# A finer order list for a gated linear attention fused with a Fourier-mix block, on one core

## The chip, the cores and the metric

The kernel runs on 1 core of one Trainium2 chip. The metric is the device time of one execution in microseconds (us). Three runs of the kernel before gave 525.32, 524.19 and 524.56 us, median 524.56.

A core has five engines that run at the same time, each through its own queue in order: PE (TensorE, matrix products into PSUM; its weight loads are shown as PEld), DVE (VectorE), ACT (ScalarE), POOL (GpSimd) and SP, which issues most of the DMA transfers. An engine waits for another one only at a semaphore, where it needs that engine's result or a buffer that the other still uses.

## The reference

Inputs q, k, v and f_logit have shape (4, 8, 768, 48): batch, heads, tokens, channels. The weights are 384 x 1536 and 1536 x 384, given in float64.

```python
# attention: a gated outer-product state for each head
f = 1 / (1 + exp(-f_logit))
for t in range(S):
    state = f[t, :, None] * state + outer(k[t], v[t])
    y[t] = q[t] @ state
# bridge: (B, H, S, D) -> x of (B, S, H*D) = (4, 768, 384)
mixed = real(fft(fft(x, axis=tokens), axis=channels))
u = x + mixed
un = (u - mean(u)) / sqrt(var(u) + 1e-6)        # over the channels
out = u + relu(un @ w_ch1) @ w_ch2
```

## The kernel before

**Units and batches.** The attention is cut into 16 units: unit u is batch u // 4 and the head pair u % 4. Each batch then has its Fourier part and its two-layer part. Work of neighbouring batches overlaps: while PE works on the layers of one batch, the units of the next one run beside them.

**The order is written out by hand.** The program text holds one string, ORDER, of words separated by blanks. A loop at the end of the kernel takes them one by one, and each word issues one piece of work. Nothing reorders it afterwards: an engine's queue is the sequence in which the words issued its instructions. The order of words on different engines doesn't matter in itself, only through waits. Most pieces come from Python generators: a word advances its generator to the next `yield`. The words are:

- a number n: the next step of unit n's attention. The steps are: gate logarithms (ACT, L372 and L373); the cumulative scan (DVE, L379); exponentials (ACT, L383, L384 and L387); two multiplications (DVE, L391 and L392); score products (PE, L400); the causal mask (DVE, L404); products of the diagonal parts with the values and the far scores with their copy (PE, ACT L579); the other value products and the state products `ds` (PE, L559 and L599); the state scan (DVE, L607); the state's share of the output (PE, L616) with five copies (ACT, L625 to L629); transposes `yt` (PE, L636) with two copies into x (ACT, L640 and L641); and the folds of x for the Fourier part (DVE, L663 to L669, for later head pairs L678 to L687 as well, of which `se` at L681 is the first transform's operand).
- Kn: the key transposes of unit n (PE, L538, with one copy on ACT).
- Fb: the next step of batch b's Fourier part: four transforms along the tokens, `z` (PE, L724, with copies on ACT), then three mixes along the channels, `mix` (PE, L743), added to x by DVE.
- Hb: the next step of its normalization: moments (DVE), and `turn`, a subtraction (DVE, L779), three transposes (PE, L782) and a copy (ACT, L783).
- Pb: the next step of the two layers. For batch 0 the first layer is 36 plain groups `up` (L871), with one pair's second layer `po` (L880). For batches 1 to 3 each of three pairs of token blocks has 15 products of the first layer (`hidden`, PE L840). DVE first makes sums of the inputs (L814) for some of them; the result goes to h by a copy on ACT (L847) or an accumulation on DVE (L849), and some end in a relu (ACT, L851). Eight steps of the second layer follow, `fx` and `fz` (PE, L894).
- r, R (three at once): a DMA of a raw weight block into one of three buffers. C: its conversion to float32 (ACT L281, DVE L283 and L284, POOL L285), 24 in all. W and B: sums of weight blocks (DVE). V and c: the raw weight blocks are read again and their smallest magnitudes found (DVE, L344). M: a verdict from these and from the scans' extremes, on which a second, slower path would run; the inputs here don't take it.
- Ln with letters: DMA loads of unit n's f, k, q and v. I, Z, i: constants. T: the DMA loads of the Fourier tables (SP, and an indirect load on POOL, L226). S: their sorting (POOL, L240 to L252; L240 and L241 finish the table that `z` reads).
- D: eight spare bfloat16 products on PE (L192). Their result isn't used and they wait for no other engine's data except once for a constant.

**Buffers.** PSUM tiles of the attention come from a ring of two (tag sc), those of the Fourier part and of most of the layers from another ring of two (tag f), and all units share one output bank y, so a unit's first value products wait for the copies of the unit before.

Of the kernel before, what the change touches and what calls it, by code (L numbers as in the profile page):

```python
# [12 lines left out]
C = 128  # L13
# [70 lines left out]
def kernel(  # L84
# [23 lines left out]
    R = 64 + D  # L108
# [256 lines left out]
    def attention(u, x_all):  # L365
# [18 lines left out]
        nc.scalar.activation(W, W, AF.Exp)  # L384
        te = te_t[u % 2][:R]
# [5 lines left out]
        nc.vector.tensor_tensor(Q, Q, g, ALU.mult)  # L391
        nc.vector.tensor_tensor(g, W, K, ALU.mult)  # L392
# [149 lines left out]
    def outputs(u, x_all, AT, Q, K, te, T=None):  # L542
# [26 lines left out]
        if te is not None:  # L569
# [3 lines left out]
            for i in range(NCH // 2):  # L573
                for p, c in ((0, i), (64, i + 3)):
                    for r in range(2):
                        nc.tensor.matmul(ps[p:p + 64, r, i * 64:i * 64 + 64],
                                         lhsT=K[ROWS[r], c * C:c * C + 64],
                                         rhs=Q[ROWS[r], c * C + 64:(c + 1) * C], start=True, stop=True)
            nc.scalar.copy(far, ps[:, :, :NCH // 2 * 64].rearrange("p r (c t) -> p r c t", t=64))  # L579
# [534 lines left out]
```

## Time and profile before

| | |
|---|---|
| median of the runs | 524.56 us (524.19 to 525.32) |
| the profiled execution, first to last instruction | 526.3 us |
| PE busy | 494.9 us (94%) |
| DVE busy | 378.3 us (72%) |
| ACT busy | 218.4 us (42%) |
| POOL busy | 58.8 us (11%) |
| first product of the first transform | 59.54 us |
| last DVE instruction of the last conversion ends | 117.6 us |
| last product ends | 519.4 us |
| mean granted PE clock | 0.974 |

The profile is one execution, recorded by the hardware. Its span, 526.3 us, is 1.7 us over the median of the timed runs. In a row of the timeline stand the start, the duration, the engine, the line of the program, the operation, its tiles and shapes, and in brackets the idle time of the engine before it with what ended it. PE's ends are modelled, so that products that overlap count as busy throughout.

### The profile page before, as it was taken

The numbers are of one execution on the slowest core, as the hardware profiler recorded it, in microseconds if no ns is written. First come the engines' busy times: TensorE is split into PE (matmuls) and PEld (weight loads), VectorE is DVE, ScalarE is ACT, GpSimd is POOL, SyncE is SP. The second block draws the span as 40 slices with busy tenths as digits, with TensorE's granted clock in tenths as the row PEclk, the third lists the DMA queues.
The fourth block names the chain that finished last, engine by engine and source line by source line (L and its number), as shares of the span: only waits on it lengthen the run. The fifth ranks groups of instructions, "written<-read, shape, count | busy, mean of one in ns | idle before, by whom it ended". The sixth has DMA issues, their size and how long they took to land.

```text
span 526.3 us, 13807 instructions
## 1 busy us (share of the span) xinstructions
PE 494.9 (94%) x5854; PEld 453.4 (86%) x5854; DVE 378.3 (72%) x746; ACT 218.4 (42%) x520; POOL 58.8 (11%) x85
## 2 busy tenths in 40 slices
PE   5878599999999999999999999999999999999994
PEld 4757388866899889999999999999999999999994
DVE  3598989989955368688588776779776667465571
ACT  5567368656331542453435523550431404031220
POOL 3045033551001000000001000000001000010100
PEclk9789699999999999999999999999999999999998
DMA  8957837575010230103212012120610312220200
GB/s 222 268 147 206 210 109 214 161 221 158 6 55 30 68 97 17 54 21 114 77 55 84 1 55 72 46 63 23 206 43 15 107 47 81 83 91 8 84 11 27
DMA packets 20650, 48.15 MB, mean 91 GB/s; under 512 B 3426, under 2 KB 6179, under 8 KB 20579
## 3 DMA queue, kind: packets, MB, share of 16 engines
q1 hardware_dynamic: 19474, 43.63, 29.5%
q0 software_dynamic: 1104, 3.54, 1.8%
q8 instruction: 48, 0.79, 0.6%
q14 instruction: 24, 0.19, 0.1%
HBM read 42.44 MB, written 4.72 MB: 90 GB/s over the span
## 4 chain that ended last, share of the span: by engine, by line
PE 87%; DVE 6%; issue 2%; ACT 2%; DMA 1%; POOL 0%; SPq 0%; DVEq 0%; ACTq 0%
PE ub L840 23%; PE fx L894 16%; PE fz L894 11%; PE up L871 9%; PE z L724 5%; PE y L559 4%; PE mix L743 3%; PE y L616 2%; PE sc L400 2%; PE ds L599 2%; PE po L880 2%; PE yt L636 2%; PE pt L782 1%; PE st L538 1%; PE y L192 1%
## 5 line engine op out<-in xcount | busy, mean ns | idle before, releaser
L849 DVE TENSOR_TENSOR h<-h,ub 128x512 f32<-128x512 f32 x81 | 55.2, 687 | 33.5 <-PE ub L840 24.5
L692 POOL DMA_INDIRECT out_dram<-x,place x16 | 16.4, 1024 | 357.6 <-DVE x L944 224.3
L847 ACT ACTIVATE h<-ub 128x512 f32<-128x512 f32 x54 | 31.9, 591 | 42.3 <-PE ub L840 42.3
L871 PE MATMUL up<-unT,w 128*128 128x256 f32 x216 | 49.4, 382 | 0.0
L840 PE MATMUL ub<-wide,w 128*128 128x128 f32 x360 | 45.0, 276 | 2.3 <-DVE wide L814 2.3
L894 PE MATMUL fx<-block,h 128*128 128x192 f32 x264 | 46.9, 328 | 0.0
L894 PE MATMUL fx<-w,h 128*128 128x192 f32 x264 | 45.5, 327 | 0.0
L840 PEld LDWEIGHTS ub<-wide,w 128*128 128x128 f32 x360 | 42.4, 192 | 3.4 <-PE pt L782 1.3
L871 PEld LDWEIGHTS up<-unT,w 128*128 128x128 f32 x216 | 40.1, 190 | 5.9 <-ACT h L873 0.4
L851 ACT ACTIVATE h<-h 128x512 f32<-128x512 f32 x45 | 28.4, 631 | 38.1 <-DVE h L849 37.7
L894 PEld LDWEIGHTS fx<-block,h 128*128 128x128 f32 x264 | 43.2, 190 | 0.5 <-DVE x L911 0.2
L894 PEld LDWEIGHTS fx<-w,h 128*128 128x128 f32 x264 | 42.7, 190 | 0.4 <-issue 0.2
L285 POOL TENSOR_TENSOR w<-w,raw 128x384 uint32<-128x384 uint32 x24 | 29.4, 1228 | 72.3 <-DVE w L284 39.1
L840 PE MATMUL ub<-unT,w 128*128 128x128 f32 x288 | 37.0, 275 | 0.0
L840 PEld LDWEIGHTS ub<-unT,w 128*128 128x128 f32 x288 | 34.6, 192 | 0.0
L783 ACT COPY unT<-pt 128x384 f32<-128x384 f32 x24 | 11.4, 484 | 46.8 <-PE pt L782 46.6
L840 PE MATMUL ub<-unT,wide 128*128 128x128 f32 x216 | 29.1, 278 | 0.0
L840 PE MATMUL ub<-wide 128*128 128x128 f32 x216 | 28.6, 275 | 0.1
L873 ACT ACTIVATE h<-up 128x256 f32<-128x256 f32 x36 | 13.9, 385 | 33.6 <-PE up L871 22.0
L840 PEld LDWEIGHTS ub<-unT,wide 128*128 128x128 f32 x216 | 26.4, 192 | 0.5
L840 PEld LDWEIGHTS ub<-wide 128*128 128x128 f32 x216 | 26.3, 192 | 0.3 <-PE ub L840 0.3
L379 DVE TENSOR_TENSOR_SCAN W<-g,bound 112x768 f32<-112x768 f32 x12 | 21.0, 1747 | 6.7 <-ACT g L373 6.7
(194 smaller groups left out, 1000.1 us busy)
## 6 DMA issues: line engine op xcount, KB each, us to landing
raw<-in_w_ch_dram SPq DMA_DIRECT2D x24, 384.0 KB, 5.1
v<-in_v_dram SPq DMA_DIRECT2D x16, 288.0 KB
k<-in_w_ch_dram SPq DMA_DIRECT2D x12, 384.0 KB, 3.4
g<-in_w_ch_dram SPq DMA_DIRECT2D x12, 384.0 KB, 3.3
k<-in_qkf_dram SPq DMA_DIRECT2D x14, 288.0 KB
g<-in_qkf_dram SPq DMA_DIRECT2D x12, 288.0 KB, 3.5
q<-in_qkf_dram SPq DMA_DIRECT2D x12, 288.0 KB, 3.3
wide<-in_qkf_dram SPq DMA_DIRECT2D x10, 288.0 KB, 4.7
```

What stands on the lines that cost most here:

```text
L285: nc.gpsimd.tensor_tensor(bits, bits, lo, ALU.add)
L379: nc.vector.tensor_tensor_scan(W, g, bound[:R], 0.0, ALU.add, ALU.min)
L559: nc.tensor.matmul(y[FILL[g], c // 3, c % 3 * C + t.start:c % 3 * C + t.stop], lhsT=vals[rows, o:o + (64 if g == 0 else D)], rhs=weights, ...
L692: nc.gpsimd.indirect_dma_start(out=out.rearrange("b s d -> (b s) d"), out_offset=bass.IndirectOffsetOnAxis(ap=place[:, b, i:i + 1], axis=0 ...
L724: nc.tensor.matmul(z[:, cols], lhsT=src[:, j, lo:hi], rhs=tab[:, t, T % 2, cols], start=(i == 0), stop=(i == len(parts) - 1), skip_group_c ...
L743: nc.tensor.matmul(mix[:, o], lhsT=zz[:rows_of[T], T, PLACES[c]], rhs=cd[:rows_of[T], T, :NQ - odd], start=(i == 0), stop=(i == 1))
L840: nc.tensor.matmul(chains[chain][:, m * 128:(m + 1) * 128], lhsT=block(w)[:, m * 128:(m + 1) * 128], rhs=tokens(a), start=(new and m == 0) ...
L847: nc.scalar.activation(out, got, kind, scale=1.0 if how == "=+" else -1.0)
L849: nc.vector.tensor_tensor(out, out, got, ALU.add if how == "+" else ALU.subtract)
L851: nc.scalar.activation(out, out, AF.Relu)
L871: nc.tensor.matmul(pp[:, :256], lhsT=w1[:, kt, m * 128:(m + 1) * 128], rhs=unT[:, kt], start=(kt == 0), stop=(kt == 2))
L894: nc.tensor.matmul(out, lhsT=h[:, m], rhs=blocks[i][:, m], start=(start and m == 0), stop=(m == H - 1), skip_group_check=True)
```

## The change

Two things change, and nothing of what is computed does.

**More yields.** Fourteen lines with `yield` are added, and one call becomes `yield from turn(step)`, so that many steps are cut in two or more. An attention unit has 19, 20 or 22 steps in place of 12 or 13, F 13 in place of 7, H 14 in place of 8, and P1 to P3 96 in place of 69. Two of the cuts, for example: the exponentials of a unit are parted from those of its block ends, and the subtraction of `turn` from its transposes. In the second path the count of steps taken from the normalization is adapted.

**A new list.** ORDER is replaced. The description says 969 words in place of 720; a count of the diff gives 964. Besides following the finer steps, it puts the words in another sequence. Of the spare words D it has 16 in place of 21: seven in place of eight ahead of the first score products, two in place of six between unit 0's state products and unit 1's scores, and five between the last transposes of unit 3 and F0, where there was none. T and S stand right in front of the first F0; M stands 33 words from the end in place of 8.

```diff
 ORDER = (
-    "L0f Z I 0 L0q L2q D D L1f L0k D 0 D 0 i D 1 L2f 2 0 D D D L0v 0 L1k K0 D 0 0 D L1q 0 1 D r 1 L3fk D "
-    "D D L1v 2 0 L2k 1 D r r D 1 2 1 3 3 0 C K1 1 2 0 C 1 L3q 2 1 3 C L2v 2 r K2 L4fk 3 L3v L5fk 1 2 1 D "
-    "T 2 0 4 3 D C S 1 2 5 3 D 2 3 2 4 K3 3 D L5qv L4qv 5 4 3 2 3 L6fk 3 2 3 5 R 3 F0 F0 4 6 F0 L6qv F0 C "
...
-    "V P3 P3 c P3 V P3 c P3 c P3 P3 V c c P3 P3 P3 P3 P3 P3 M P3 P3 P3 P3 P3 P3 P3 P3"
+    "L0f 0 Z I L1f 1 D D 0 0 0 D D D L0q i D D L0k L2f 2 0 0 0 0 L0v 0 0 1 2 L1q L3fk L1k K0 r 0 L2q L1v "
+    "1 L2k 1 1 0 D 3 D 1 1 0 0 2 0 K1 C 1 1 1 2 2 3 0 1 2 0 0 3 1 1 2 L3q 3 3 L2v r 2 1 1 r 3 2 2 r C K2 "
+    "L4fk 2 0 C 2 2 C 3 3 2 4 1 2 L3v 4 1 1 L4qv 2 2 2 1 3 3 4 K3 3 3 D 2 D L5fk 5 3 3 3 4 4 3 5 3 D D 4 "
+    "D 2 D 4 D K4 3 3 3 3 5 3 T S F0 F0 F0 F0 4 4 4 L5qv 5 5 R C C 5 C L6qv F0 F0 F0 H0 K5 F0 5 4 H0 L6fk "
...
+    "P3 P3 P3 P3 c c c P3 P3 P3 c V c P3 M P3 P3 P3 P3 P3 P3 P3 P3 P3 P3 P3 P3 P3 P3 P3 P3 P3 P3 P3 P3 P3 "
+    "P3 P3 P3 P3 P3 P3 P3 P3 P3 P3 P3 P3"
 )
...
         nc.scalar.activation(W, W, AF.Exp)
+        yield
         te = te_t[u % 2][:R]
...
         nc.vector.tensor_tensor(Q, Q, g, ALU.mult)
+        yield
         nc.vector.tensor_tensor(g, W, K, ALU.mult)
...
+            yield
             nc.scalar.copy(far, ps[:, :, :NCH // 2 * 64].rearrange("p r (c t) -> p r c t", t=64))
             yield
...
             diagonal(lo, hi)
+            yield
         ps = ps_a.tile([128, 2, 512], F32, tag="sc", name=f"ds{u}")
...
                              skip_group_check=True)
+        yield
         yT = p2.tile([128, S], F32, tag="yT", name=f"yT{u}")[:R]
...
             nc.tensor.transpose(ps[:, c * 128:c * 128 + R], to[:, i], ident[:R, :R])
+        yield
         x = x_all()
...
             nc.vector.tensor_scalar(un, x[:, c], mv[:, c, 0:1], rstd[:, c:c + 1], ALU.subtract, ALU.mult)
+            yield
             pt = ps_f.tile([128, 512], F32, tag="f", name=f"pt{b}_{c}")
...
-                    turn(step)
+                    yield from turn(step)
...
             mix = mixed(c)
+            yield
             nc.vector.tensor_tensor(by2(x[:, c]), rising(mix, NQ), by2(x[:, c]), ALU.add)
             moments(c)
             deviation(slice(c, c + 1))
+            yield
             nc.vector.tensor_tensor(by2(x[:, c + 3]), falling(mix, NQ), by2(x[:, c + 3]), ALU.add)
...
                 add(tokens(i), tokens(one), tokens(two), sign)
+            if made:
+                yield
             new = chain not in opened
...
             if complete and not first:
+                yield
                 nc.scalar.activation(out, out, AF.Relu)
             yield
...
-                for _ in range((3, 3, 2)[j]):
+                for _ in range((5, 5, 4)[j]):
                     next(behind[b], None)
```

The remaining three added yields cut the folds of x.

More of the change, by code (lines that the diff above doesn't have):

```diff
@@ L801, in fnet @@
             deviation(slice(c, c + 1))
+            yield
             nc.vector.tensor_tensor(by2(x[:, c + 3]), falling(mix, NQ), by2(x[:, c + 3]), ALU.add)
@@ L834, in hidden @@
                 add(tokens(i), tokens(one), tokens(two), sign)
+            if made:
+                yield
             new = chain not in opened
@@ L850, in hidden @@
             if complete and not first:
+                yield
                 nc.scalar.activation(out, out, AF.Relu)
```

37 rows, old and new, of the table ORDER are left out of this document.

## The prediction

> **What bounds the kernel now.** I read the page's head first, then the busy time in five stages that I cut at three marks: the first product of the first transform (59.5 us), the last conversion of a weight block (117.5 us) and the last product (519.4 us).
>
> ```profile
> span 526.3 us, 13807 instructions
> PE 494.9 (94%) x5854; PEld 453.4 (86%) x5854; DVE 378.3 (72%) x746; ACT 218.4 (42%) x520; POOL 58.8 (11%) x85
> ```
>
> ```profile
> 0.00:26.00 26.00, 17.14 (x357) 15.90 (x361) 11.17 (x13) 15.28 (x24) 4.80 (x29) 0.87 0.95 247
> 26.00:59.50 33.50, 22.63 (x595) 18.67 (x587) 30.74 (x57) 21.51 (x53) 13.35 (x20) 0.83 0.75 198
> 59.50:117.50 58.00, 57.04 (x917) 45.22 (x917) 51.76 (x90) 37.36 (x100) 23.10 (x19) 0.95 0.60 169
> 117.50:519.40 401.90, 398.03 (x3998) 373.61 (x3997) 284.27 (x589) 144.28 (x343) 17.50 (x17) 1.00 0.21 62
> 519.40:526.30 6.90, 0.03 (x1) 0.00 (x0) 0.36 (x1) 0.00 (x0) 0.00 (x0) 0.75 0.16 48
> ```
>
> The columns of the second fence are the stretch, its length, the busy time of PE, PEld, DVE, ACT and POOL, the granted clock, the DMA share and GB/s. From 117.5 us on PE is busy 398.0 of 401.9 us at full clock, so an order of words can win at most 3.9 us there, however it is laid. Before 59.5 us PE waits, and its busy time there is partly the spare products. DVE is what fills up: 11.17 of the first 26 us, but 30.74 of the next 33.5. The transform starts when DVE has made its operand, so the head is a DVE queue with holes at its front. Here are the holes, and the operand:
>
> ```profile
> 6.48 1.76 DVE L379 TENSOR_TENSOR_SCAN W<-g,bound 112x768 f32<-112x768 f32 x1 [6.48 <-ACT g L373]
> ...
> 9.41 0.96 DVE L391 TENSOR_TENSOR q<-q,g 112x768 f32<-112x768 f32 x1 [0.97 <-ACT g L383]
> ...
> 12.62 1.05 DVE L404 COPY_PREDICATED at<-causal,sc 128x768 f32<-128x768 uint32 x1 [1.20 <-PE sc L400]
> ...
> 20.23 0.76 DVE L607 TENSOR_TENSOR_SCAN stt<-ds,te 112x288 f32<-112x288 f32 x1 [2.82 <-PE ds L599]
> ...
> 25.96 1.04 DVE L404 COPY_PREDICATED at<-causal,sc 128x768 f32<-128x768 uint32 x1 [3.08 <-PE sc L400]
> ```
>
> ```profile
> 51.50 0.76 DVE L607 TENSOR_TENSOR_SCAN stt<-ds,te 112x288 f32<-112x288 f32 x1 [1.35 <-PE ds L599]
> ...
> 58.98 0.46 DVE L681 TENSOR_TENSOR se<-xs 128x285 f32<-128x285 f32 x1
> ```
>
> The page's wait list names no releaser for the first transform product ("issue"); the operand se ends at 59.44 us and the product starts at 59.54, so I read it as that wait. The 3.08 us hole has a cause that the change touches: the product it waits for stands behind six words of spare products in PE's queue.
>
> ```profile
> 20.11 4.93 PE L192 MATMUL y<-bound 128*128 128x128 bf16 x48
> ...
> 24.97 0.93 PE L400 MATMUL sc<-q,g 48*64 48x64 f32 x48
> ```
>
> **The change, part by part.** It adds and removes no computation. The list holds 964 words by my count of the diff (the title's 969 doesn't agree with it). Each generator's words match its new yields (19, 20 or 22 for a unit, 13 for F, 14 for H, 96 for P1 to P3), so no step is dropped. What changes is each engine's order, and 16 words of spare products stand in place of 21. Only the order on an engine counts, because another engine sees a word only through waits.
>
> *Head, up to se.* In both lists the same DVE work stands ahead of se: the six scans of units 0 to 5, the four units' products, masks, state scans and folds, and four weight conversions. The new list adds the two multiplications of unit 4:
>
> ```profile
> L391 DVE TENSOR_TENSOR q<-q,g 112x768 f32<-112x768 f32 x12 | 11.4, 950 | 6.0 <-ACT g L383 6.0
> ...
> L392 DVE TENSOR_TENSOR g<-W,k 112x768 f32<-112x768 f32 x11 | 10.5, 959 | 0.8
> ```
>
> Work: 11.17 + 30.74 = 41.9 us now, 41.9 + 1.9 = 43.8 us then. DVE's idle time is 59.5 - 41.9 = 17.6 us. Of it 6.48 + 0.97 + 1.20 = 8.65 us stay, since unit 0 still goes scan, exponentials, multiplications, scores, mask with nothing of another unit ready in between. The other three holes, 2.82 + 3.08 + 1.35 = 7.25 us, lose their cause: unit 0's state scan now stands behind unit 1's two multiplications, two words of spare products in place of six stand ahead of unit 1's scores, and unit 3's state scan stands behind four fold words of units 1 and 2. The rest, 17.6 - 8.65 - 7.25 = 1.7 us, I leave. For new waits the bounds are 0 and 7.25 us (all come back elsewhere); I take 1.5, because the second stretch above, where DVE had several units to choose from, has 2.8 us of holes in 33.5, half of which is the 1.35 already counted. Transform start: 43.8 + 8.65 + 1.7 + 1.5 = 55.7 us (54.2 to 61.4).
>
> *Tables.* T and S now stand right in front of F0. On SP this puts the four loads of q4 and v4 ahead of the tables, two of 288 KB and two smaller ones:
>
> ```profile
> v<-in_v_dram SPq DMA_DIRECT2D x16, 288.0 KB
> ...
> q<-in_qkf_dram SPq DMA_DIRECT2D x12, 288.0 KB, 3.3
> ```
>
> That is under 4 x 288 = 1152 KB, at 198 GB/s under 6.0 us. On POOL the indirect load now follows the fourth conversion.
>
> ```profile
> 37.28 1.15 POOL L226 DMA_INDIRECT tab<-in_seq_tab_dram,back  x1 [0.30 <-POOL back L225]
> 43.34 1.02 POOL L285 TENSOR_TENSOR w<-w,raw 128x384 uint32<-128x384 uint32 x1 [4.91 <-ACT raw L281]
> 46.56 1.48 POOL L240 COPY pair<-tab 128x8 f32<-128x8 f32 x1 [2.20 <-DMA wave<-in_dim_tab_dram]
> 48.10 0.21 POOL L241 COPY tab<-pair 128x8 f32<-128x8 f32 x1
> ```
>
> The table is whole at 48.3 us now, and with 6.0 us of loads ahead at 54.3, still under 55.7. If the fourth conversion on POOL is no later than its present 43.34, the indirect load starts at 44.4 at the earliest, takes at most the 9.3 us between its issue and L240 today (46.56 - 37.28), and with 1.7 us for L240 and L241 the table is whole at 55.4. So the move costs nothing, with little to spare; every microsecond by which that conversion is later than 43.6 delays the transform by one.
>
> *Clock in the transform.* The transform's products take 8.37 us now. The same 28 products of the last batch take 3.92 + 1.32 = 5.2 us:
>
> ```profile
> 59.54 8.37 PE z L724 x28
> ...
> 369.22 3.92 PE z L724 x20
> ...
> 381.18 1.32 PE z L724 x8
> ```
>
> ```profile
> 51.70:55.10 3.40, 1.94 (x32) 1.40 (x29) 3.19 (x9) 1.83 (x7) 1.68 (x4) 1.00 1.03 240
> 55.10:58.50 3.40, 0.06 (x1) 0.00 (x0) 2.99 (x10) 2.67 (x5) 0.00 (x0) 0.52 1.01 279
> ...
> 65.40:68.80 3.40, 3.40 (x66) 2.60 (x65) 2.53 (x4) 3.26 (x14) 0.00 (x0) 0.99 0.02 7
> ```
>
> The clock is at half from 55.1 us on and full again in the row from 65.4, so 8.37 - 5.24 = 3.1 us are its doing. It fell after a stretch in which PE was busy 1.94 of 3.40 us. The new list puts five spare words, unit 4's scores and its key transposes between unit 3's last transposes and the transform:
>
> ```profile
> 51.38 0.62 PE L192 MATMUL y<-bound 128*128 128x128 bf16 x8
> ...
> 54.37 0.79 PE L636 MATMUL yt<-ident,yT 112*128 112x112 f32 x6 [1.15 <-ACT yT L629]
> ...
> 71.49 0.70 PE L538 MATMUL st<-ident,g 112*128 112x112 f32 x5
> ```
>
> That is 5 x 0.62 + 0.93 + 0.70 = 4.7 us of PE work in a gap that is 4.4 us today (55.16 to 59.54) and gets no spare word. The spare words wait for nothing, though: if DVE is later than the list supposes they run out early and PE idles again. So I count half of the 3.1 us as won.
>
> The Trainium skill ("TensorE: Matmul & The Clock Gate", section "HAM oscillation — how this bites in real kernels") asks for no idle gap over some 3.4 us. By that rule the filled gap would keep full clock, and the sum would come 1.5 us lower. The row ending at 55.1 us speaks against it: that stretch has no gap near 3.4 us, and the clock fell at its end.
>
> *Transform to last conversion (59.5 to 117.5 us now).* Both engines are close to their limit here, so the longer of two sums decides. The list ahead of the last conversion differs in little: gone to the head are unit 4's multiplications (DVE 1.9), scores and key transposes (PE 1.6); one spare word (PE 0.6) is gone; one weight sum (DVE 0.69, row below) and unit 5's last transposes (PE 0.8) come later; three of DVE's subtractions at L779 (DVE 1.4 in all) and two of their transposes (PE 0.8) come sooner. PE: 57.04 - 1.6 - 0.6 - 0.8 + 0.8 = 54.8, less 3.1 at full clock = 51.7, with today's 1.0 idle 52.7. DVE: 51.76 - 1.9 - 0.7 + 1.4 = 50.6, at today's busy share (51.76 / 58.0 = 0.89) 56.7. Raw blocks are fetched three ahead, and near the end DVE waits for them:
>
> ```profile
> 114.96 0.69 DVE L812 SCALAR_TENSOR_TENSOR wide<-w 128x512 f32<-128x512 f32 x1
> ...
> 116.61 0.36 DVE L283 TENSOR_SCALAR w<-raw 128x384 uint32<-128x384 uint32 x1 [0.96 <-DMA raw<-in_w_ch_dram]
> 117.00 0.56 DVE L284 SCALAR_TENSOR_TENSOR w<-raw,w 128x384 uint32<-128x384 uint32 x1
> ```
>
> The new list keeps the fetches as close behind the buffers' release, so this wait stays. Between 52.7 and 56.7 I take 55.5, nearer DVE's end: half the clock loss is back on PE's side (54.2) and 1.3 us are left to waits like this one. Last conversion: 55.7 + 55.5 = 111.2 us in place of 117.5, a gain of 6.3 us.
>
> *The long stretch.* The PE work behind that mark is the same in both lists, to 0.1 us. Finer words let a subtraction, an accumulation or a copy stand a word earlier than the product that needs it, so part of the 3.9 us of idle PE can go; new waits can come. Bounds: 3 us less, 1.5 us more. I take 1.0 less.
>
> *The tail.* The last eight P3 words follow each other as before, so the 6.9 us behind the last product stay. The verdict word M stands 33 words from the end in place of 8. The last re-read block is issued behind the use of the block four earlier; some 6 us of PE work lie between, against 3.3 us for such a load (row below); if that cover went, DVE would wait about a microsecond there. I count M as nothing.
>
> ```profile
> g<-in_w_ch_dram SPq DMA_DIRECT2D x12, 384.0 KB, 3.3
> ```
>
> Sum: 526.3 - 6.3 - 1.0 = 519.0 us of span. The runs' median is 524.56, 1.7 under the profiled span; the same difference gives **517.3 us**.
>
> **Rivals.**
> *Full clock and no DVE wait in the second stage.* PE's sum of 52.7 us holds: 55.7 + 52.7 = 108.4, a gain of 9.1, with the long stretch's 1.0: 514.5 us. For it: DVE needs only 50.6 us for that stage, and the filled gap. Against: DVE was never over 0.92 busy in a stage of the head. By the Trainium skill's clock rule this case would be the likelier one.
> *The holes come back.* DVE waits 7.25 us in other places, since DMA is 0.95 busy in the first 26 us and cannot deliver sooner: start at 61.4, last conversion at 116.9, gain 0.6 + 1.0: 523.0 us. For it: the first unit's chain is unchanged, and the weight conversion moved to the front waits for a raw block behind eleven loads. Against: the 3.08 us hole was PE's doing, not DMA's.
> *Slower: finer words part what belonged together.* The relu (L851) that ends a hidden block was emitted right behind its accumulation; now another unit's word may stand between on ACT, a unit's five output copies for example, 0.37 + 0.38 + 0.28 + 0.29 + 0.20 = 1.5 us:
>
> ```profile
> 53.27 0.37 ACT L625 COPY yT<-y 112x254 f32<-112x254 f32 x1 [0.78 <-PE y L616]
> ...
> 54.11 0.20 ACT L629 COPY yT<-y 112x4 f32<-112x4 f32 x1
> ```
>
> The second-layer products are queued behind that relu on PE. There are nine such blocks. From five on (5 x 1.5 = 7.5 us) the head's gain is gone; with seven, 10.5 us lost against 6.3 won, the time is 528.8 us. For it: PE has only 3.9 us of idle there, so every new wait shows. Against: ACT is 36% busy (144.28 of 401.9 us), and the last four blocks have no unit's copies beside them.
>
> **How the numbers follow.** Chances: forecast 0.46, full clock 0.25, holes back 0.17, slower 0.12. The forecast's own range is 514 to 520.5 (start 54.2 to 57, second stage 54 to 56.7, long stretch -2.5 to +0.5). For 8 in 10 it reaches down to the second case with the long stretch at its best, 54.2 + 52.7 and 3.0 less, 511.0, and up past the third case: 511 to 524.5. A change of 0.2% (about 1 us) is what a measurement of this kernel can tell from none. Faster: the first two cases and two thirds of the third less a little, 0.80; the same 0.09; slower 0.11.
>
> **What would show it.** Head: DVE's waits before L607 and L404 between 17 and 26 us shrink, and z's first product starts near 55.7; a start after 59 makes the head's step wrong. Clock: PE's idle time right before z, and z in 5.4 to 8.4 us. Second stage: the last L284 ends near 111. Long stretch: idle PE between that mark and the last product, 3 us or less; 8 us or more is the slower rival. Tables: z waiting for L241 would put the wait on POOL. The prediction fails altogether if the last product is not 4 to 10 us earlier than 519.4.

## The result, and the profile after

The kernel after takes **517.31 us** (median of four runs, 515.84 to 521.55) beside 524.94 us for the kernel before in the same session (524.19 to 525.90): a ratio of **0.9866, 95% interval 0.9823 to 0.9909**. The forecast was 517.3 us. A second series of the same kernel, later, had 519.1 us and 0.9892 (0.9856 to 0.9928). So the list is worth 5.7 to 7.0 us by the two ratios; their intervals leave 3.8 to 9.3. Three single runs of kernels below (1919.67, 642.22 and 531.45 us) were in a slow state and stand in no ratio.

The forecast's total was right. Its shares were not, and the stages show that. The stages of the kernel after, cut at the same marks as before (columns: stretch, length, busy time of PE, PEld, DVE, ACT, POOL, granted clock, DMA share, GB/s):

```profile
span 519.8 us, 13729 instructions
...
0.00:26.00 26.00, 13.38 (x352) 11.92 (x356) 16.30 (x19) 17.01 (x30) 7.05 (x30) 0.97 0.94 233
26.00:59.26 33.26, 27.24 (x614) 23.21 (x614) 26.70 (x53) 19.73 (x47) 14.01 (x19) 0.76 0.85 234
59.26:115.72 56.46, 54.64 (x869) 43.18 (x869) 49.67 (x90) 38.26 (x102) 23.31 (x20) 1.00 0.57 162
115.72:513.04 397.32, 393.65 (x3984) 371.98 (x3984) 282.55 (x587) 142.61 (x343) 18.06 (x17) 1.00 0.21 63
513.04:519.80 6.76, 0.00 (x0) 0.00 (x0) 0.36 (x1) 0.00 (x0) 0.00 (x0) 0.73 0.16 48
```

This execution was the longest of its four (521.55 us timed). The second series' profile is the shortest of its eight (517.08 us); its stages, cut in the same way:

```profile
0.00:26.00 26.00, 14.18 (x363) 12.61 (x364) 16.65 (x19) 17.03 (x30) 6.77 (x30) 0.99 0.96 234
26.00:55.91 29.91, 23.16 (x601) 19.92 (x600) 26.69 (x53) 18.15 (x45) 14.39 (x19) 0.90 0.93 243
55.91:111.04 55.13, 54.02 (x868) 43.19 (x869) 50.89 (x90) 39.34 (x104) 23.63 (x20) 1.00 0.59 171
111.04:508.35 397.31, 394.24 (x3986) 371.98 (x3984) 282.55 (x587) 142.63 (x343) 18.06 (x17) 1.00 0.21 63
```

Two things are to be seen. The long stretch is the same to 0.01 us in both (397.3, before 401.9); the last conversions of the two differ by 4.7 us, 3.4 of it ahead of z and 1.3 behind it. So one profile says much about the long stretch and little about the head. And the long stretch shrank by 4.6 us, where the prediction expected 1.0; 1.4 us of that is work that stands ahead of the mark now, as is worked out further below.

The head of the kernel after, DVE's waits up to the transform, in total by line (in the first profile, then in the second):

```profile
DVE W L386 <- ACT g L380: 6.1, 1, 6.1
DVE stt L618 <- PE ds L610: 3.1, 2, 1.8
DVE eo L676 <- ACT x L654: 2.4, 3, 1.9
DVE at L413 <- PE sc L409: 1.4, 2, 1.2
DVE q L399 <- ACT g L390: 0.9, 1, 0.9
```

```profile
DVE W L386 <- ACT g L380: 6.3, 1, 6.3
DVE eo L676 <- ACT x L654: 1.7, 1, 1.7
DVE at L413 <- PE sc L409: 1.2, 1, 1.2
DVE q L399 <- ACT g L390: 0.9, 1, 0.9
DVE stt L618 <- PE ds L610: 0.7, 1, 0.7
```

The first unit's three waits stand (L386, L399, 1.2 us of L413), as the prediction had it. The 2.82, 3.08 and 1.35 us holes are gone. What came back elsewhere (waits for a state product, for x) is 5.5 us (L618 and L676) in one execution and 2.4 us in the other.

The transform starts a tenth of a microsecond behind its operand, as before, and runs at full clock:

```profile
58.70 0.46 DVE L696 TENSOR_TENSOR se<-xs 128x285 f32<-128x285 f32 x1
```

```profile
55.42 0.93 PE L409 MATMUL sc<-q,g 48*64 48x64 f32 x48
56.28 0.62 PE L199 MATMUL y<-bound 128*128 128x128 bf16 x8
56.73 0.65 PE L547 MATMUL st<-ident,g 112*128 112x112 f32 x5
59.26 1.51 PE L740 MATMUL z<-tab,se 128*95 128x385 f32 x6 [1.87 <-POOL half L257]
```

se ends at 59.16, z starts at 59.26. (The row names POOL, but L257 made nothing that z reads; in the second profile se ends at 55.81, z starts at 55.91 and the row names nobody.) z's 28 products take 5.45 us in both, 8.37 before.

### The profile page after: what moved, and what is told of

Read it like the earlier page. It is cut to its first block, busy times and chain, and to the rows that moved or that the text cites. A ratio compares the mean times of both kernels' runs of the same rounds, so it can differ in the third digit from the quotient of the medians.

```text
span 519.8 us, 13729 instructions
## 1 busy us (share of the span) xinstructions
PE 488.9 (94%) x5814; PEld 450.3 (87%) x5814; DVE 375.6 (72%) x746; ACT 217.6 (42%) x520; POOL 62.4 (12%) x85
## 4 chain that ended last, share of the span: by engine, by line
PE 82%; DMA 7%; DVE 3%; issue 2%; POOL 2%; ACT 2%; SPq 1%; DVEq 0%; POOLq 0%; ACTq 0%
PE ub L861 23%; PE fx L916 17%; PE fz L916 13%; PE up L893 8%; PE z L740 4%; DMA raw<-in_w_ch_dram 4%; PE mix L759 3%; PE y L568 3%; PE y L627 2%; PE po L902 2%; DMA k<-in_qkf_dram 2%; PE sc L409 2%; PE ds L610 2%; PE pt L799 1%; DMA tab<-in_seq_tab_dram 1%
## 5 line engine op out<-in xcount | busy, mean ns | idle before, releaser
L386 DVE TENSOR_TENSOR_SCAN W<-g,bound 112x768 f32<-112x768 f32 x12 | 21.1, 1762 | 7.5 <-ACT g L380 7.5
```

Source lines behind the costliest of these rows:

```text
L386: nc.vector.tensor_tensor_scan(W, g, bound[:R], 0.0, ALU.add, ALU.min)
```

## The experiments

All marks below are microseconds of the profiled execution of each kernel, one execution each. As the two profiles of the kernel after differ by 3.4 us in the start of z, a single row says little about that start and about the last conversion; the last column hardly varies. "P1" is the first product of batch 1's two layers (211.4 us before); up to it and behind it nearly the same work lies in every list. Each timed run was compared with runs of the kernel before on the same chip.

| kernel | ratio to before, 95% | z starts | z takes | last conversion | z to P1 | P1 to last product |
|---|---|---|---|---|---|---|
| before | 1 | 59.54 | 8.37 | 117.56 | 151.8 | 308.1 |
| after | 0.9866 (0.9823-0.9909) | 59.26 | 5.45 | 115.72 | 148.9 | 304.9 |
| after, second series | 0.9892 (0.9856-0.9928) | 55.91 | 5.45 | 111.04 | 147.6 | 304.9 |
| new to last conversion, then old | 0.9929 (0.9898-0.9960) | 56.60 | 7.13 | 113.57 | 149.9 | 307.9 |
| old to last conversion, then new | 0.9971 (0.9943-0.9999) | 59.90 | 7.87 | 117.19 | 152.8 | 304.9 |
| old to F0, then new | 1.0005 (0.9973-1.0036) | 63.82 | 7.31 | 120.23 | 148.8 | 304.9 |
| new to F0, old to last conversion, new | 0.9943 (0.9914-0.9971) | 57.06 | 5.45 | 114.25 | 152.7 | 304.9 |
| after without the five spare words | 0.9913 (0.9882-0.9944) | 57.86 | 7.13 | 115.44 | 150.0 | 304.9 |
| before with five spare words | 0.9997 (0.9972-1.0022) | 57.07 | 7.14 | 115.17 | 152.4 | 307.9 |
| before, two spare words of six | 1.0045 (1.0019-1.0072) | 56.83 | 7.47 | 116.86 | 153.9 | 307.9 |
| the same with four raw buffers | 1.0008 (0.9980-1.0036) | 60.27 | 7.29 | 116.53 | 151.7 | 307.9 |
| after, seven more spare words | 0.9900 (0.9860-0.9940) | 58.21 | 5.45 | 113.65 | 147.9 | 304.9 |
| after, four raw buffers | 0.9862 (0.9811-0.9913) | 57.14 | 5.45 | 111.15 | 146.6 | 304.9 |
| after, M late | 0.9854 (0.9812-0.9896) | 56.34 | 5.45 | 112.35 | 148.4 | 305.5 |

### Which part of the list

The list was cut at the last conversion word C; one part was taken from each sequence, with the finer steps throughout. At the joint, words that the first part had already issued were left out of the second. The kernel after ran again beside the two halves.

```diff
 # new up to the last C, then old
-"... C 7 7 H0 H0 P0 C H0 L8fk 7 9 5 5 L9qv 9 9 9 P0 P0 P0 P0 ..."
+"... C 7 7 H0 H0 P0 C 5 5 L8fk L8qv B B 7 B 9 9 B 8 P0 8 9 9 ..."
```

> The changed kernel as it is, timed again, with a second profile. Theory A (from the two traces): the transform again starts within 1 us of 59.3 us, its products take 5.4 us, the last conversion ends near 115.7, and the time is 517 us, within a band of 514 to 522. Theory B (the prediction's own steps, the first profile being a bad draw): the transform starts near 55.7, the last conversion ends near 111, the stretch behind it is about 1 us shorter than before, and the time is 515 to 517 us.

> The new list up to the last weight conversion, then everything that is left in the old list's sequence. Theory A: the head with its full clock in the transform is worth about 1.8 us by the last conversion, the long stretch's 4.6 us are not won: 523 us. Theory B: the head is worth 6.3 us, only the stretch's 1.0 is not won: 518.5 us.

> The old list up to the last weight conversion, then everything that is left in the new list's sequence. Theory A: the long stretch's 4.6 us are won without the head: 520.3 us. Theory B: only 1.0 us is won: 524 us.

The medians, all on one chip: the new part up to the last conversion alone 521.97 us, the new part behind it alone 524.5, both 519.1, before 525.73: 3.8, 1.2 and 6.6 us. The second part alone has the time of its Theory B, but not for that theory's reason. It is worth more in its own place: its stretch from P1 on is 304.9 us, 3.2 under before's. The joint hides that, because behind an old head the way from the last conversion to P1 is 95.5 us in place of 93.8. The kernel with the new part up to the last conversion has the finer steps too, and its stretch from P1 on stays at 307.9 us: what shortens it is the new sequence, not the added yields alone. The second profile of the kernel after has the head of Theory B (55.91 and 111.04) with the long stretch of Theory A (4.6 us shorter); its series' median, 519.1 us, lies in Theory A's band and above Theory B's.

The second pair was cut at the first F0 as well.

```diff
 # old up to F0, then new
-"... D 2 D 4 D K4 3 3 3 3 5 3 T S F0 F0 F0 F0 4 4 4 L5qv 5 5 R C C ..."
+"... 3 2 3 3 5 5 R 3 3 3 4 4 4 K4 F0 F0 F0 F0 4 4 4 5 C C ..."
 # new up to F0, old to the last C, new behind it
+"... D K4 3 3 3 3 5 3 T S L5qv L6fk 5 R F0 F0 6 F0 L6qv F0 C ..."
```

> The steps of the kernel after; the list takes the old sequence up to the first F0 and the new one from there on (words that the old part has issued already are left out). Theory (an earlier start of the transform is lost on the way in the old sequence, and the gain up to the last conversion is the new sequence behind F0): the transform starts near 59.5 us as before, but the last conversion comes near 115 us, and the time is 2 to 3 us under the list that is old up to the last conversion, so 0.991 to 0.994 of before. Rival (the prediction's: most of the gain is the earlier start): the last conversion comes at 116.5 us or later and the ratio is 0.995 to 0.999.

> The steps of the kernel after; the list takes the new sequence up to the first F0, the old one from there to the last conversion, and the new one behind it. Theory (as for the list with the two parts the other way round): the transform starts at 56 to 58 us, but the stretch from there to the last conversion takes 58 us or more, as with two spare words in place of six, so the last conversion comes at 115 to 117 us and the ratio is 0.994 to 0.998. Rival (the prediction's): the stretch takes 55 to 56.5 us, the last conversion comes at 112 to 113.5 us and the ratio is 0.988 to 0.991.

The second kernel answers only in part. z starts at 57.06 and runs at full clock, but from there to the last conversion it takes 57.2 us, between the rival's 55 to 56.5 and the theory's 58 or more. From z to P1 it takes 152.7 us, as long as in the five kernels with the old sequence there (151.7 to 153.9), where the new sequence takes 146.6 to 150.0. Most of that is the joint's, however: from the last conversion to P1 it takes 95.5 us, as in the other kernel with this joint (the old words up to the last conversion, then the new ones), against 92.4 in the kernel after. So 3.1 us belong to the joint, and 1.3 us (57.2 beside 55.9, the mean of the three profiles with the words of the kernel after up to there) can be the old sequence's.

The ratios put the new words ahead of F0 at 0.28% (0.9971 to 0.9943, both with this joint), about 1.5 us. The remaining 0.51% (0.9943 to 0.9892), about 2.7 us, are the new words from F0 to the last conversion and the absence of the joint together. Both differences lie within the intervals of the ratios. Which part of the head wins is not shown.

The first kernel doesn't answer: its joint has a fault. Unit 4's scores and key transposes came to stand ahead of z on PE, while the multiplications that they need stand behind se on DVE. The rows, DVE's and then PE's:

```profile
56.69 0.46 DVE L697 TENSOR_TENSOR se<-xs 128x285 f32<-128x285 f32 x1
...
60.29 0.96 DVE L402 TENSOR_TENSOR g<-W,k 112x768 f32<-112x768 f32 x1
```

```profile
61.35 1.56 PE L410 MATMUL sc<-q,g 48*64 48x64 f32 x48 [8.47 <-issue]
62.84 1.19 PE L548 MATMUL st<-ident,g 112*128 112x112 f32 x5
63.82 2.77 PE L741 MATMUL z<-tab,se 128*95 128x385 f32 x6
```

se is ready at 57.15 and z starts at 63.82: 6.7 us for three words in the wrong place. The stretch from z to P1, 148.8 us, is still that of the new sequence.

### The spare words and the clock

```diff
 # after without the five
-"... 4 4 3 5 3 D D 4 D 2 D 4 D K4 3 3 3 3 5 3 T S F0 F0 ..."
+"... 4 4 3 5 3 4 2 4 K4 3 3 3 3 5 3 T S F0 F0 ..."
 # before with five
-"... 2 3 5 R 3 F0 F0 4 6 ..."
+"... 2 3 5 R 3 D D D D D F0 F0 4 6 ..."
```

> The changed kernel without the five spare words between unit 3's last transposes and the first transform. If the spare words keep the clock (Theory A): the transform's products take about 8.4 us in place of 5.4, and the time is 3 us over the changed kernel's. If unit 4's scores and key transposes are cover enough, or the clock is set by something else: the products still take 5.4 us and the time is the changed kernel's within 1 us.

> The kernel before, with five words of spare products put right in front of its first F0, and nothing else. Theory (the clock step by itself): the five words, 5 x 0.62 = 3.1 us of PE work, fill the gap in which PE idled ahead of the transform, so the transform's 28 products take 5.4 to 6.0 us in place of 8.37, and the last conversion comes 1 to 2.5 us earlier; the time falls by 1 to 2.5 us, as the same five words were worth 1.9 us in the kernel after. Rival (the second stage is bound by DVE, not by PE): z gets shorter but the last conversion stays within 0.5 us of 117.5 and the time does not move. Second rival: the clock is decided earlier in the head, where PE idles; z stays at 7 us or more.

Without the five words the median is 521.01 us, against 519.1 for the kernel after on the same chip. That is 1.9 us, but the intervals of the two ratios overlap (0.9882 to 0.9944, 0.9856 to 0.9928), so the loss is likely and not shown. z takes 7.13 us in place of 5.45 (8.4 was expected), and the clock falls right where it fell before (three stretches of some 3.4 us, and z's first products with the gap ahead of them):

```profile
50.80:54.30 3.50, 1.85 (x55) 1.60 (x56) 3.47 (x7) 1.82 (x8) 3.50 (x4) 1.00 1.05 214
54.30:57.70 3.40, 0.62 (x5) 0.41 (x5) 3.16 (x9) 2.21 (x3) 3.07 (x8) 1.00 0.70 163
57.70:61.10 3.40, 3.24 (x9) 2.08 (x10) 3.30 (x8) 0.59 (x3) 0.70 (x1) 0.64 0.03 12
```

```profile
57.86 2.08 PE L740 MATMUL z<-tab,se 128*95 128x385 f32 x6 [2.94 <-POOL half L257]
```

The five words do not always keep the clock. The kernel with the new words up to the last conversion has them too, and z takes 7.13 us there behind a gap of 1.94 us (first row below). In the other six profiles with the new words up to F0 and the five spare ones z takes 5.45, behind gaps of 0.46 to 1.96 us. In the kernel before, with five spare words added, the gap ahead of z is 2.14 us and z takes 7.14 (second row):

```profile
56.60 1.93 PE L740 MATMUL z<-tab,se 128*95 128x385 f32 x6 [1.94 <-POOL half L257]
```

```profile
57.07 1.72 PE L725 MATMUL z<-tab,se 128*95 128x385 f32 x6 [2.14 <-issue]
```

So in the kernel before the five words bought only 1.2 us of z, z to P1 did not get shorter (152.4 against 151.8), and the time did not move (0.9997). Of the rivals, the first has its sign in the time, not in the last conversion (115.17, behind a z that starts 2.5 us earlier), and the second in z at 7 us or more. Since the clock was not kept there, the run can't tell what a full clock would be worth in the old sequence.

### Six words of spare products, or two

```diff
-"... D r 1 L3fk D D D L1v 2 0 L2k 1 D r r D 1 2 1 3 3 0 C K1 ..."
+"... D r 1 L3fk D L1v 2 0 L2k 1 r r 1 2 1 3 3 0 C K1 ..."
```

> The kernel before, with two in place of six words of spare products between unit 0's state products and unit 1's scores, and nothing else. Theory (the prediction's step for the 3.08 us hole): unit 1's mask waited for scores that stood behind the spare products; the hole at 25.96 us falls under 1 us, the transform starts about 2 to 3 us earlier than 59.5, and the time falls by 1.5 to 3 us. Rival (the spare products keep the clock up, and what they cost in place they win in speed): the hole closes, but PE's clock falls within the next 10 us and the products of units 1 and 2 take up to twice as long, so the transform starts within 1 us of 59.5 and the time is the same or longer.

The hole is smaller (unit 1's mask waits 1.20 us in place of 3.08, and unit 0's state scan 1.00 in place of 2.82), and z starts at 56.83 in place of 59.54. That looks like the prediction's reading, but the kernel before with five spare words, which keeps all six of these words, has the small hole as well, and z starts at 57.07 there. Its rows, PE's and then DVE's:

```profile
19.40 2.85 PE L193 MATMUL y<-bound 128*128 128x128 bf16 x48
```

```profile
23.37 1.04 DVE L405 COPY_PREDICATED at<-causal,sc 128x768 f32<-128x768 uint32 x1 [1.20 <-PE sc L401]
```

The six words take 2.85 us here and 4.93 in before's profile, where the granted clock was 0.54 from 17.4 to 20.8 us and 0.50 from there to 24.2; here it was 1.00 in both. The two kernels with the old words up to F0 or beyond show 2.85 and 1.20 us too. So 1.9 of the 3.08 us go with the half clock of that one execution, not with the number of the words. And two words do not make an early start: with four raw buffers, below, the same words start z at 60.27.

The kernel got **slower**, 0.45%. Why is not shown. In its profile the stage behind z grows from 58.0 to 60.0 us, and DVE waits 3.9 us for raw weight blocks in it (1.7 before). PE's clock between 26 and 40 us is 0.65 (0.81 before), but in the profile with four raw buffers, with the same words up to there, it is 0.86. The clock's row, and the last of the waits:

```profile
26.00:40.00 14.00, 10.90 (x254) 9.24 (x253) 13.15 (x24) 8.25 (x19) 5.68 (x7) 0.65 0.93 245
```

```profile
115.91 0.36 DVE L284 TENSOR_SCALAR w<-raw 128x384 uint32<-128x384 uint32 x1 [2.61 <-DMA raw<-in_w_ch_dram]
```

### The three raw buffers

Both kernels show waits for raw blocks, so the raw blocks got four buffers, cut from the same room, and one fetch more at the start of the conversions; once in the kernel after, once in the one just shown.

```diff
-        raw = pr.tile([128, 2, 3, DM // 2], U32, tag="raw", name=f"raw{i}").rearrange("p a b n -> p (a b n)")
-        raw = raw[:, :768].rearrange("p (n w) -> p n w", w=2)
+        raw = raw_words[:, i % 4 * 2 * DM:(i % 4 + 1) * 2 * DM].rearrange("p (n w) -> p n w", w=2)
...
-        t2, t3, t4 = [pr.tile([128, H, HD], F32, tag="raw", name=f"block{i}") for i in range(3)]
+        t2, t3, t4 = [raw_t[:, i].rearrange("p (h n) -> p h n", n=HD) for i in range(3)]
 # list of the kernel after
-"... L5qv 5 5 R C C 5 C ..."
+"... L5qv 5 5 R r C C 5 C ..."
```

> The kernel after, with four buffers for the raw weight blocks in place of three (cut from the same 13.5 KB of a partition) and one fetch more issued behind the word R, so that every later fetch is one block further ahead. Theory (the end of the second stage is set by the cycle of three buffers: fetch 3 to 5 us, conversion on ACT, DVE and POOL, next fetch): DVE's waits for raw blocks, 5.2 us in the profile of after and 2.4 in that of its second run, fall under 1 us, the last conversion comes 1.5 to 3 us earlier for the same start of the transform, and the time is 515.5 to 517.5 us, 0.982 to 0.986 of before. Rival (DMA's rate sets it: DMA is 1.01 busy from 110 to 118 us): the waits stay above 2 us and the ratio is that of after, 0.987 to 0.990.

> The kernel before with two in place of six words of spare products, and with the four raw buffers and one fetch more ahead. Theory (the 2.7 us by which the transform started earlier with two words were lost to the cycle of three raw buffers and the 2.6 us wait at its end): the transform starts near 57 us, DVE's waits for raw blocks (3.85 us there) fall under 1 us, the last conversion comes at 113 to 115 us, and the ratio to before is 0.992 to 0.996. Rival (they were lost to PE's lower clock and to waits between engines): the raw waits fall, the last conversion stays at 116 us or later, and the ratio is 0.999 to 1.005.

DVE's waits from 57 to 118 us, in the kernel after and then with four buffers:

```profile
DVE w L290 <- DMA raw<-in_w_ch_dram: 5.2, 5, 1.8
DVE W L386 <- ACT g L380: 1.4, 1, 1.4
```

```profile
DVE W L388 <- ACT g L382: 1.3, 1, 1.3
DVE x L819 <- PE mix L761: 0.2, 1, 0.2
```

The waits for raw blocks are gone, and z to P1 is the shortest of all, 146.6 us. So the cycle of three buffers, not DMA's rate, made those waits. In time it is 518.16 us and 0.9862, just outside what the theory expected (515.5 to 517.5 us); the interval covers both series of the kernel after, so a gain over it is not shown. With the old sequence the waits are gone too, and the time is that of before (1.0008), as its rival said. Beside the same kernel with three buffers (1.0045) the intervals overlap, so it is not shown that they cost anything there either. That profile's transform started at 60.27, a late draw of the head.

### A warmer head

```diff
-"... 0 K1 C 1 1 1 2 2 3 0 1 2 0 0 3 1 1 2 L3q 3 3 L2v r 2 1 1 r ..."
+"... 0 K1 D D C 1 1 1 2 2 3 0 D 1 2 0 0 3 1 1 2 L3q 3 3 L2v r 2 1 D D 1 r ..."
 # and one D each ahead of unit 2's output and behind unit 1's last transposes
```

> The kernel after, with seven more words of spare products in its head, at places where PE idled in the profile: two behind K1, one behind unit 0's last output, two behind unit 1's, one ahead of unit 2's output, one behind unit 1's last transposes. Theory (the half clock between 24 and 41 us doubles PE's links of the units' chains and so opens DVE's holes of 1.85 + 1.83 us): the granted clock stays above 0.9 from 26 to 45 us, the holes shrink, the transform starts near 55.5 us, and the time is at or under 517 us, 2 us under the kernel after in the same call of runs. Rival: the spare words stand in front of products that DVE waits for, seven times up to 0.62 us, the transform starts at 57 us or later and the time is that of the kernel after or 1 to 4 us more.

The rival holds. The clock is 1.00 from 26 us on, and yet DVE waits 14.4 us up to z (11.4 in the second profile of the kernel after), the transform starts at 58.21 and the time is 0.9900, that of the kernel after:

```profile
26.00:45.00 19.00, 14.98 (x462) 12.80 (x463) 13.73 (x26) 11.24 (x29) 5.26 (x7) 1.00 0.87 238
```

```profile
DVE eo L677 <- ACT x L655: 3.3, 3, 1.7
DVE stt L619 <- PE ds L611: 1.6, 2, 1.1
```

So keeping the clock up by spare words does not buy an earlier start. Whether the half clock opens those holes is not settled by it, since the seven words themselves stand in front of products that DVE waits for. Seven profiles have the same words up to 45 us: the two of the kernel after, and those with M late, with four raw buffers, without the five spare words and of the two kernels with the new words up to F0 or the last conversion. Among them the clock from 26 to 40 us tells nothing: 0.62 goes with a start at 59.26, and 0.64 with one at 56.34. The clock from 40 to 45 us does go with the start, with one exchange: 0.50 (59.26 and 57.86), 0.70 (57.06), 0.87 (57.14), 0.95 (56.60), 0.99 (56.34) and 1.00 (55.91). Which of the two makes the other, if either does, stays open.

### The verdict word

```diff
-"... P3 P3 P3 c V c P3 M P3 P3 P3 ..."      (33 words from the end)
+"... P3 P3 P3 c V c P3 P3 P3 P3 ... P3 M P3 P3 P3 P3 P3 P3 P3 P3"
```

> The kernel after, with the verdict word M put back 8 words from the end in place of 33; nothing else changes. Theory (formed from the traces of before and after): M's work made PE wait where it stood late, 2.1 us between two products, while 33 words from the end it falls in a wait of 0.9 us that the pair of blocks has anyway. So the stretch from P1's first product to the last product grows from 304.8 to 306.1 us (+1.3, at most +1.5), with a gap of about 2.1 us back near the end. The prediction's own step (M moved costs nothing, wins nothing): 304.8 within 0.3 us.

P1 to the last product grows from 304.87 to 305.50: 0.63 us, between theory and prediction. M late is a wait of its own on PE; M early lengthens a wait that the pair of blocks has anyway (1.2 us in place of 0.8). PE's waits from 440 us on with M late, then in the kernel after:

```profile
PE ub L862 <- DVE wide L834: 1.5, 2, 0.8
PE turned L992 <- DVE most L990: 0.7, 1, 0.7
```

```profile
PE ub L861 <- DVE wide L833: 1.8, 2, 1.2
```

The time (518.84 us, 0.9854) can't tell 0.6 us.

## Why the prediction was right, and where it was not

**The bound of 3.9 us was read wrongly.** That "an order of words can win at most 3.9 us there" took PE's busy time for work. The long stretch fell by 4.6 us, and PE's idle time in it only from 3.9 to 3.7 (3.1 in the second profile). It is the busy time that fell, by 4.4 us (3.8). There are two parts to that.

The first is no gain. "The PE work behind that mark is the same in both lists" is wrong: between the last conversion and P1 the new list has 13 products fewer, 4 of the second layer (`po`) and 9 transposes (`turn`), because they stand ahead of the last conversion now. This is 1.4 of the 4.6 us. Before and after:

```profile
117.56:211.36 93.80, 93.26 (x963) 80.94 (x963) 68.06 (x124) 37.16 (x96) 5.74 (x5) 1.00 0.22 63
```

```profile
115.72:208.13 92.41, 91.21 (x950) 79.39 (x951) 66.77 (x120) 35.87 (x96) 5.63 (x5) 1.00 0.22 62
```

The second part is won. From P1 to the last product, where both kernels have the same 3034 products, before and after:

```profile
211.36:519.43 308.07, 304.77 (x3035) 292.66 (x3034) 216.15 (x466) 107.12 (x247) 11.76 (x12) 1.00 0.20 62
```

```profile
208.13:513.04 304.91, 302.44 (x3040) 292.59 (x3034) 215.79 (x468) 106.74 (x247) 12.43 (x12) 1.00 0.21 63
```

PE's busy time is 2.3 us less for the same products (the x counts also those that reach over an edge). A product's bar is longer than its distance to the next one in the same group (275 ns beside 112 ns for the products of hidden), so a late start of up to some 0.16 us hides under the bar before it. Counted from the starts alone (each distance to the next start less the most frequent one of its shape, where over 30 ns), products start late 194 times for 19.3 us in this stretch before, and 158 times for 15.2 us after. Of the 4.2 us fewer, 2.4 are late starts under 0.2 us (186 and 155 of them), most of which no wait list shows; the other 1.7 are longer ones, eight before and three after. The count is rough, as the stretch itself got only 3.2 us shorter. The verdict word's place accounts for 0.63 us of the 3.2.

So the term was mis-sized: 1.0 us was forecast with 3 at most, the mark shows 4.6, and on equal work it is 3.2 (3.0 against the four other profiles with the old words there, 307.9 us).

**The head's gain was too high.** The last conversion came at 115.72, 111.04 and 112.35 us in the three profiles with the same words up to there, 113.0 on the mean: 4.5 us less than before's profile, not 6.3. Even 4.5 is much, because before's profile was a long execution (next paragraph): of the 5.7 to 7.0 us that the runs give, the 4.6 of the long stretch leave 1.1 to 2.4 us by the last conversion, or 2.5 to 3.8 us by P1, as an estimate. The working held in part: DVE's work ahead of the transform is 16.30 + 26.70 = 43.0 us (predicted 43.8). In the second profile its idle time is 12.6 us (55.91 - 16.65 - 26.69; predicted 8.65 + 1.7 + 1.5 = 11.9), and start and last conversion are 55.91 and 111.04, the predicted 55.7 and 111.2 almost to the tenth. In the first profile DVE's idle time is 16.3 us, so that the new waits are 5.9 us in place of the 1.5 that the sum took, within its bounds of 0 and 7.25. By the prediction's sign for this step, a start after 59 makes it wrong, the first profile (59.26) speaks against it, and the second and the one with M late (55.91 and 56.34) do not. Its last sign, a last product 4 to 10 us earlier, holds in the first profile (6.4) and not in the second (11.1).

**The two lists' profiles were both draws.** Each profiled run's own time was 1.75 us over its span (521.55 and 519.8, 517.08 and 515.3). By that, before's profile of 526.3 us belongs to an execution of 528.0 us, above all runs shown with it. The prediction took 1.7 us off the span where 1.75 us come on top. That and the head's 1.8 us were made up for by the long stretch: 526.3 - 4.5 - 4.6 + 1.75 = 518.95 us, which fits the second series' 519.1 and lies 1.6 us over the first's median, within its spread. The forecast's 517.3 has three terms off (+1.8, -3.6, +3.5) that nearly cancel; that it met the first median so closely is luck. Its own range, 514 to 520.5, is also narrower than the terms behind it allow (512.8 to 521.3, all low or all high).

**Holes.** Right as far as none of the three is left in the two profiles of the kernel after. Their sizes and the cause of the largest were not: 3.08 us was put down to six spare words, and with the same six words at full clock it is 1.20 us. The prediction took one execution's half clock for a property of the list. In the kernels with the old words there unit 0's state scan waits 0.97 to 2.82 us and unit 3's 1.24 to 3.68. The two-of-six run starts z 2.7 us before before's profile and is slower all the same, so an early start in one profile does not carry over to the time.

**Clock.** Half of 3.1 us was counted as won; in both profiles of the kernel after nearly all of it was (5.45 beside the floor of 5.24). The run without the five words is 1.9 us longer, within the noise of the two. The rule of the Trainium skill ("TensorE: Matmul & The Clock Gate", section "HAM oscillation — how this bites in real kernels"), no idle gap over some 3.4 us, would have had the filled gap right; but without the five words PE's longest gap there was the 2.94 us of the row above and the clock still fell to 0.64, so the rule alone would have called that safe, and the gap of 1.94 us above as well. The row against it was read rightly.

**Second stage.** 55.5 us was put between PE's 52.7 and DVE's 56.7; it took 56.5, 55.1 and 56.0. The "waits like this one" were 5.2 and 2.6 us for raw blocks in the first two; with four buffers and none of them the stage took 54.0 us. The rival without DVE waits, 52.7, was reached in no profile.

**Tables.** Right. The table is whole when L248 ends, at 53.3 us, 6 us ahead of z:

```profile
50.38 0.18 POOL L247 COPY pair<-tab 128x8 f32<-128x8 f32 x1 [4.82 <-DMA tab<-in_seq_tab_dram,back]
50.63 2.67 POOL L248 COPY tab<-pair 128x8 f32<-128x8 f32 x1
```


**M and the tail.** M was worth 0.63 us, not nothing. The tail is 6.8 to 7.0 us, as before.

**The slower rival** did not show: PE waits for no relu from P1 on; its waits there are for L833's sums alone. The sign that the prediction named for the long stretch, 3 us of idle PE or less, came out at 3.7 and 3.1 and told little, since busy bars hide late starts.

## What to carry to other kernels

PE's busy bars are not work: before saying what an order can still win, compare the starts of successive products with their usual distance. A mark that ends a stage must have the same work behind it in both kernels; here 13 products had crossed it. Before a hole is put down to the instructions ahead of it, look at the clock in that stretch, and in a second profile: the same six words took 4.93 and 2.85 us. And put a profile beside its own timed run before its span is used as the starting point: here a draw 3.5 us above the median.

## What the hardware showed that was not expected

The length of PE's idle gap alone does not decide whether the clock falls: it fell after gaps of 1.94, 2.14 and 2.94 us ahead of z, and held over gaps of 1.87 and 1.96. Where spare products held it at 1.00 from 26 us on, the head got no shorter. And the part of the kernel behind P1 hardly varies (304.87 to 304.88 us in eight profiles with the new words there, 307.88 to 307.89 in four with the old ones and 308.07 in before's), while the start of z in one program moves by 3.4 us between two executions.
